# Dense K, Q and output rows, and VectorE's share of the exponentials, in an attention and gated-MLP kernel on one Trainium2 core

## The chip, the cores and the metric

The kernel runs on one core of a Trainium2 chip. The metric is the time on the device, in microseconds (us), of one execution. A profiled execution also leaves a trace with the start and length of every instruction on TensorE (PE), VectorE (DVE), ScalarE (ACT), GpSimd (POOL) and SyncE (SP).

## The reference

A layer of 2048 rows and 640 columns, in bf16: the layer norm of x feeds an attention with 32 heads of 20 columns, and a gated MLP of 1728 columns; both results are joined with x.

```python
xn = layernorm(x)                                       # 2048 x 640
q, k, v = split(xn @ wqkv)                              # 32 heads of Dh = 20
p = softmax(q @ k.T * 20**-0.5)                         # 2048 x 2048 for each head
s = (p @ v).reshape(S, D) @ wo
h = sigmoid(xn @ w_gate) * (xn @ w_up)
g = silu(h @ w_down)
out = x + s * g
```

## The kernel before, in words

**Passes and banks.** The queries are cut into four blocks (`qc`) of 512, the heads into eight groups (`g`) of four. A pair (qc, g) is a pass; there are 32. In a pass, each of the four heads has 16 key tiles of 128, so a pass has 64 banks: a bank is one 128x512 tile of scores, in one bank of PSUM. All 2048 banks must go through an exponential.

The four heads of a group lie on partitions 0, 32, 64 and 96 of `kT_all[:, g, :]` and `qT`, each with 21 rows that count: row 0 carries a bound that is subtracted from the scores, rows 1 to 20 the head's columns. `score` (L874) multiplies 32 rows of the two.

**Who does the exponentials.** `issue` (L928) takes three banks for ScalarE, then two, then three, and so on, in two PSUM sets `sc0` and `sc1`; `act_exp` (L896) turns each such chunk into `p` by one activation (L901). With each chunk one more bank may go to VectorE: `issue` takes one of two PSUM banks (`misc0`, `misc1`, under the name `spare`) if one is free, VectorE's backlog is under 2.5 us (`D_BACKLOG`), and the pass has more than `NEEDED` = 6 banks left (12 in the last pass). `dve_exp` (L906) does that bank in four instructions on 512 columns: `bits` (L912, PSUM to `dy`), `square` (L917, `dy` to `du`), `cube` (L921, `du` to `du`) and `power` (L925, `du` and `dy` to `p`). There is one buffer `du` and two `dy`.

**The other work.** The same two `misc` banks hold the results of all other matmuls (`work`). These are jobs, written as generators:

- `k_job(g, c)`: K of group g, keys of block c: five matmuls with the weights `wkp`, in which each head's 20 columns are padded to 32 (L108); VectorE writes `kT_all` with a 1 in row 0 (L475) and takes the largest magnitude (L121). The last of a group makes the weights of the bound (L118, L115).
- `q_job(qc, g)`: five matmuls with `wqp`, padded in the same way (L143); VectorE takes the magnitudes from PSUM (L127); a sixth matmul adds the bound (L501); VectorE writes `qT` (L506).
- `v_job`, and for the MLP `gateup_job` (L541, L554, tanh on ScalarE L548, product on VectorE L558) and `down_job` (L576).
- `out_job`: the output rows, eight matmuls of 320 columns for each half row tile, one for each group, from `oTs[qc, g]` and the padded `wo_pad` (L614); `part_job` (L646) does the same for six groups of the last query block; the last two groups come at the very end (`out_mm`, L1088).

After a pass, `normalise` copies the sums out of PSUM (L667), sends the denominators through DRAM for the reciprocal (L668 to L684, on POOL's queue) and writes `oT` (L696).

**What sets the order.** The order on every engine is written out by a planner inside the kernel: it keeps a clock for PE (`pe`), queues for ScalarE and VectorE with a cost for each instruction, and a due time (in banks) for each job. `INTO` says what it adds on PE when that engine turns to scores, to PV products or to jobs: 160, 100 and 100 ns. It stops the jobs when the scores are due: `until = max(free, dry - AHEAD) - into`, where `free` is the time at which ScalarE has left the set, `dry` the last moment that keeps ScalarE busy, and `AHEAD` is 80 ns. The chip then runs these orders, each engine in its own, held by semaphores. SP's queue loads `wg`, `wu`, `gqr` and the weights, in program order. When nothing else is due, a multiplication with zeros (`zero_add`) keeps PE running.

Of the kernel before, what the change touches and what calls it, by code (L numbers as in the profile page):

```python
# [14 lines left out]
P = 128  # L15
# [6 lines left out]
V_CHUNKS = ((0, 16), (16, 32))  # L22
OBUFS, WB = 1, 2
# [16 lines left out]
def kernel(  # L40
# [46 lines left out]
    mk_all = const.tile([P, NG, 4], FP32, name="mk_all")  # L87
    mk = const.tile([P, NG], FP32, name="mk")
    bound = const.tile([P, NG, P], BF16, name="bound")
# [7 lines left out]
    wqp = persist.tile([P, KD, HEAD, 32], BF16, name="wqp")  # L97
    wo_pad = persist.tile([P, NG, D], BF16, name="wo_pad")
# [4 lines left out]
    wkp = ep.tile([P, KD, HEAD, 32], BF16, name="wkp")  # L103
    wv = ep.tile([P, KD, D], BF16, name="wv")

    def k_matmuls(ps, g, cols):
        for kd in range(KD):
            nc.tensor.matmul(ps, lhsT=wkp[:, kd, GH * g:GH * g + GH, :].rearrange("p h e -> p (h e)"),  # L108
                             rhs=xnT[:, kd, cols],
                             start=(kd == 0), stop=(kd == KD - 1))  # L110
            yield

    def k_bound(g):
        k_most(g)
        nc.vector.tensor_scalar(out=bound[:, g, :], in0=esum, scalar1=mk[:, g:g + 1], scalar2=None, op0=ALU.mult)  # L115

    def k_most(g):
        nc.vector.tensor_reduce(out=mk[:, g:g + 1], in_=mk_all[:, g, :], axis=AXISX, op=ALU.max)  # L118

    def k_max(src, g, c):  # L120
        nc.vector.tensor_reduce(out=mk_all[:, g, c:c + 1], in_=src, axis=AXISX, op=ALU.max,  # L121
                                apply_absolute_value=True)

    def q_abs(ps):
        absq = wk.tile([P, QC], BF16, tag="absq", bufs=1, name="absq")
        high = ps.bitcast(U16).rearrange("p (q two) -> p q two", two=2)[:, :, 1]
        nc.vector.tensor_scalar(out=absq.bitcast(U16), in0=high, scalar1=0x7FFF, scalar2=None,  # L127
                                op0=ALU.bitwise_and)
        return absq
# [11 lines left out]
    def q_matmuls(ps, cols, g):  # L141
        for kd in range(KD):
            nc.tensor.matmul(ps, lhsT=wqp[:, kd, GH * g:GH * g + GH, :].rearrange("p h e -> p (h e)"),  # L143
                             rhs=xnT[:, kd, cols],
                             start=(kd == 0), stop=(kd == KD - 1))
            yield

    V_SETUP = 4
    qTs = {}
    with tc.tile_pool(name="setup", bufs=1) as sp, \
            tc.tile_pool(name="ps0", bufs=1, space=bass.MemoryType.PSUM) as ps0:
        x_sb = sp.tile([P, TT, D], BF16, name="x_sb")
        wk_raw = sp.tile([P, KD, D], BF16, name="wk_raw")
        wq_raw = sp.tile([P, KD, D], BF16, name="wq_raw")
# [20 lines left out]
        load_w(wk_raw, 1)  # L178
        load_x(12, 4)
        load_w(wq_raw, 0)  # L180
# [7 lines left out]
        nc.vector.memset(wkp[:, :, GH:HEAD, 1 + Dh:32], 0.0)  # L188
        for w in (wkp, wqp):
            nc.gpsimd.memset(w[:, :, 0:GH, 0:1], 0.0)  # L190
            nc.gpsimd.memset(w[:, :, 0:GH, 1 + Dh:32], 0.0)
# [13 lines left out]
        def pad_copy(dst, raw, g0, g1):  # L205
            nc.gpsimd.tensor_copy(
                out=dst[:, :, GH * g0:GH * g1, 1:1 + Dh],
                in_=raw[:, :, GH * g0 * Dh:GH * g1 * Dh].rearrange("p k (h e) -> p k h e", e=Dh))
# [38 lines left out]
        def k_mm(c):  # L247
            kps[c] = ps0.tile([P, 512], FP32, tag="k", bufs=KBUFS, name="ps_k")
            for _ in k_matmuls(kps[c], 0, slice(c * 512, (c + 1) * 512)):
                pass  # L250
# [16 lines left out]
        def q_mm():  # L267
            first["ps"] = ps0.tile([P, 512], FP32, tag="q", bufs=1, name="ps_q")
            for _ in q_matmuls(first["ps"], slice(0, QC), 0):
                pass  # L270

        def q_bound():
            nc.tensor.matmul(first["ps"], lhsT=bound[:, 0, :], rhs=first["abs"], start=False, stop=True,
                             skip_group_check=True)

        def q_evict():
            qT = wk.tile([P, QC], BF16, tag="qT", bufs=2, name="qT")
# [20 lines left out]
        op(("wkp",), "POOL", 0.52, ["wk"], lambda: pad_copy(wkp, wk_raw, 0, 1))  # L298
        ends["wk"], ends["wq"], ends["wv"] = 10.8, 14.7, 16.7
        op(("wqp",), "POOL", 0.52, ["wq"], lambda: pad_copy(wqp, wq_raw, 0, 1))  # L300
        for c in range(4):
            op(("k", c), "PE", 1.3, [("xnT", 4 * c + i) for i in range(4)] + [("wkp",)]
               + ([("kmax", c - KBUFS), ("kadd", c - KBUFS)] if c >= KBUFS else []), lambda c=c: k_mm(c), 0.2)
            op(("kmax", c), "DVE", 0.64, [("k", c)], lambda c=c: k_max(kps[c], 0, c))
            op(("kadd", c), "ACT", 0.57, [("kmax", c)], lambda c=c: k_add(c), 0.6 * (c == 3))
        op(("kmost",), "DVE", 0.2, [("kmax", c) for c in range(4)], lambda: k_most(0))
        op(("kbound",), "ACT", 0.3, [("kmost",)],
           lambda: nc.scalar.activation(out=bound[:, 0, :], in_=esum, func=ACT.Identity, scale=mk[:, 0:1]))
# [30 lines left out]

        nc.gpsimd.memset(wkp[:, :, GH:HEAD, 0:1], 0.0)  # L340
        pad_copy(wkp, wk_raw, 1, 2)
        nc.gpsimd.memset(wqp[:, :, GH:HEAD, 0:1], 0.0)
        nc.gpsimd.memset(wqp[:, :, GH:HEAD, 1 + Dh:32], 0.0)
        pad_copy(wqp, wq_raw, 1, 2)
        pad_copy(wkp, wk_raw, 2, NG)
        pad_copy(wqp, wq_raw, 2, NG)
        nc.gpsimd.memset(v_all[:, :, HH:HEAD, 0:1], 1.0)
        nc.gpsimd.memset(wo_pad.rearrange("p g d -> p (g d)"), 0.0)
# [11 lines left out]
    INTO = {"score": 160.0, "pv": 100.0, "fill": 100.0}  # L360
# [101 lines left out]
    kb_cells = {0: Cell(0.0)}  # L462
# [7 lines left out]
    def k_job(g, c):  # L470
        cols = slice(c * 512, (c + 1) * 512)
        held, ps = yield "bank",
        for _ in k_matmuls(ps, g, cols):
            yield "mm", MM5
        k_cells[g, c] = dve.add(630.0, [Cell(pe[0] + PE_OUT)], lambda: nc.vector.tensor_scalar(  # L475
            out=kT_all[:, g, cols], in0=ps, scalar1=e0[:, 0:1], scalar2=None, op0=ALU.add), 1)
        give_bank(held, k_cells[g, c])
        most = dve.add(620.0, [k_cells[g, c]], lambda: k_max(kT_all[:, g, cols], g, c), 2)
        kb_cells.setdefault((g, "max"), []).append(most)
        if c == 3:  # L480
            kb_cells[g] = dve.add(400.0, kb_cells[g, "max"], lambda: k_bound(g), 2)
# [11 lines left out]
    def q_job(qc, g):  # L493
        yield "known", lambda: kb_cells.get(g)
        held, ps = yield "bank",
        for _ in q_matmuls(ps, slice(qc * QC, (qc + 1) * QC), g):
            yield "mm", MM5
        made = {}
        got = dve.add(600.0, [Cell(pe[0] + PE_OUT)], lambda: made.update(absq=q_abs(ps)), 0)
        yield "wait", [got, kb_cells[g]]  # L500
        nc.tensor.matmul(ps, lhsT=bound[:, g, :], rhs=made["absq"], start=False, stop=True, skip_group_check=True)  # L501
        yield "mm", MM5

        def evict():
            qT = wk.tile([P, QC], BF16, tag="qT", bufs=2, name="qT")
            nc.vector.tensor_scalar(out=qT, in0=ps, scalar1=q_scale, scalar2=e_one[:, 0:1], op0=ALU.mult, op1=ALU.add)  # L506
            qTs[qc, g] = qT

        q_cells[qc, g] = dve.add(600.0, [Cell(pe[0] + PE_OUT)], evict, 0)
        give_bank(held, q_cells[qc, g])  # L510
# [53 lines left out]
    def down_job(tt):  # L564
        c, t4 = divmod(tt, QC // P)
        yield "known", lambda: len(h_cells.get(c, [])) == NFT and (tt < 2 or tt - 2 in gq_cells)
# [22 lines left out]
        def finish():  # L589
            last = c == NQC - 1  # L590
            gq = glu[0].tile([P, D], FP32, tag="gqr", bufs=4, name="gq") if last else d2
# [12 lines left out]
    def out_job(tt):  # L604
# [3 lines left out]
        gqr = glu[0].tile([P, D], FP32, tag="gqr", bufs=4, name="gqr")  # L608
        nc.sync.dma_start(out=gqr, in_=gq_dram[tt, :, :])
        landed = Cell(pe[0] + 3000.0)  # L610
        for h in range(2):
            held, pss = yield "bank",
            for g in range(NG):
                nc.tensor.matmul(pss[:, 0:HALF], lhsT=oTs[qc, g][:, t4 * P:(t4 + 1) * P],  # L614
# [537 lines left out]
```

## Time and profile before

| | us |
|---|---|
| median of three runs before (915.34 to 917.61) | 915.73 |
| the profiled execution | 916.7 |
| its span, first to last instruction | 914.8 |
| from the span's start to the first exponential | 32.4 |
| from the first to the end of the last exponential | 864.3 |
| from there to the end of the span | 18.2 |
| ScalarE busy, in the span | 880.2 |
| VectorE busy, in the span | 837.8 |
| TensorE matmuls busy, in the span | 805.1 |
| mean granted TensorE clock | 0.994 |

A busy share is the union of an engine's instructions. Two instructions of ScalarE overlap at their ends, so what one costs is read from start to start, not from its length. The trace has 1813 banks of scores under the name `sc`, for ScalarE, in 363 chunks of three and 362 of two, and 235 under the name `spare`, for VectorE.

### The profile page before, as it was taken

How to read it: one execution, taken by the hardware profiler on the slowest of the kernel's cores; microseconds unless marked ns; L12 is line 12 of the kernel's file. 1: busy time of each engine (PE TensorE's matmuls, PEld its weight loads, DVE VectorE, ACT ScalarE, POOL GpSimd, SP SyncE). 2: the span in 40 equal slices, each digit the busy share in tenths (PEclk: the TensorE clock that was granted, in tenths of full speed). 3: DMA queues.
4: the chain of work that ended last, by engine and by line, in shares of the span. 5: the costliest groups of instructions: out<-in, count | busy, mean ns of one | idle time of the engine just before them, and what ended most of it. 6: DMA issues, size and time to landing. Idle time of an engine off the chain costs nothing.

```text
span 914.8 us, 16028 instructions
## 1 busy us (share of the span) xinstructions
PE 805.1 (88%) x6027; PEld 274.3 (30%) x6027; DVE 837.8 (92%) x1424; ACT 880.2 (96%) x845; POOL 167.7 (18%) x307
## 2 busy tenths in 40 slices
PE   5898889988888998898889998998899999989995
PEld 2332223322222233322223333222233322223333
DVE  8799999998999999999999999999889967989995
ACT  6989999999999999999999999999999999999992
POOL 7601111011111111211111112111011221011121
PEclk9999999999999999999999999999999999999997
DMA  6070000002222112322221132322102333220003
GB/s 223 22 227 14 13 14 14 2 14 56 49 64 46 32 59 70 51 56 56 57 49 28 52 100 35 66 62 57 38 20 85 79 49 71 45 56 21 13 17 84
DMA packets 91901, 49.50 MB, mean 54 GB/s; under 512 B 78548, under 2 KB 86132, under 8 KB 91696
## 3 DMA queue, kind: packets, MB, share of 16 engines
q1 hardware_dynamic: 81616, 32.37, 14.0%
q0 software_dynamic: 10208, 16.11, 7.8%
q8 instruction: 47, 0.77, 0.3%
q14 instruction: 30, 0.25, 0.1%
HBM read 40.74 MB, written 9.03 MB: 54 GB/s over the span
## 4 chain that ended last, share of the span: by engine, by line
ACT 64%; issue 16%; DVE 10%; PE 8%; DMA 1%; POOL 0%; SPq 0%; DVEq 0%; ACTq 0%; POOLq 0%
ACT p L901 59%; ACT tnh L548 3%; PE sc L879 3%; DVE dy L912 2%; DVE du L917 1%; DVE du L921 1%; PE work L541 1%; DVE p L925 1%; PE oacc L999 1%; DVE stats L214 1%; PE work L133 1%; PE work L554 1%; ACT td L587 1%; DMA x_sb<-in_A_x_dram 0%; PE work L143 0%
## 5 line engine op out<-in xcount | busy, mean ns | idle before, releaser
L901 ACT ACTIVATE p<-sc 128x1536 bf16<-128x1536 f32 x725 | 840.5, 1399 | 6.6 <-PE oacc L999 5.2
L879 PE MATMUL sc<-qT,kT_all 32*128 32x512 bf16 x1813 | 283.1, 382 | 76.7 <-ACT p L901 70.4
L879 PEld LDWEIGHTS <-kT_all 32*128 32x128 bf16 x2048 | 90.9, 90 | 320.0 <-issue 310.3
L912 DVE TENSOR_SCALAR dy<-spare 128x512 f32<-128x512 f32 x235 | 160.8, 684 | 26.0 <-PE spare L879 23.9
L917 DVE SCALAR_TENSOR_TENSOR du<-dy 128x512 f32<-128x512 uint16 x235 | 161.3, 686 | 4.6
L925 DVE SCALAR_TENSOR_TENSOR p<-du,dy 128x512 uint16<-128x512 f32 x235 | 161.0, 685 | 4.0
L921 DVE SCALAR_TENSOR_TENSOR du<-du,dy 128x512 f32<-128x512 f32 x235 | 161.1, 685 | 3.5
L999 PE MATMUL oacc<-p,v_all 128*21 128x512 bf16 x2048 | 157.4, 383 | 0.0
L668 POOL DMA_DIRECT2D den_dram<-oev x31 | 18.0, 582 | 397.1 <-DVE oev L667 387.8
L879 PE MATMUL spare<-qT,kT_all 32*128 32x512 bf16 x235 | 90.1, 383 | 0.0
L576 PE MATMUL work<-wd,hT 128*128 128x320 bf16 x448 | 85.4, 302 | 0.3 <-DVE dy L912 0.2
L541 PE MATMUL work<-xnT,wg 128*128 128x512 bf16 (+1 forms) x280 | 81.2, 383 | 1.0 <-DVE dy L912 0.3
L554 PE MATMUL work<-xnT,wu 128*128 128x512 bf16 (+1 forms) x280 | 76.7, 381 | 1.8 <-DVE dy L912 0.9
L684 POOL DMA_DIRECT2D rl<-rec_dram x124 | 62.1, 513 | 55.0 <-DMA rec_dram<-den 46.4
L576 PEld LDWEIGHTS <-hT 128*128 128x128 bf16 x448 | 35.7, 97 | 46.9 <-issue 35.3
L999 PEld LDWEIGHTS <-v_all 128*21 128x21 bf16 x2048 | 29.7, 90 | 63.3 <-issue 62.3
L143 PE MATMUL work<-xnT,wqp 128*128 128x512 bf16 x155 | 43.9, 382 | 2.5 <-DVE dy L912 2.0
L548 ACT ACTIVATE tnh<-work 128x512 bf16<-128x512 f32 (+1 forms) x56 | 44.3, 791 | 0.0
L558 DVE SCALAR_TENSOR_TENSOR hT<-tnh,work 128x512 bf16<-128x512 bf16 (+1 forms) x56 | 38.0, 679 | 5.4 <-ACT tnh L548 3.9
L678 POOL DMA_DIRECT2D rec_dram<-den x31 | 17.0, 550 | 132.2 <-DVE den L677 132.2
L108 PE MATMUL work<-xnT,wkp 128*128 128x512 bf16 x140 | 39.8, 383 | 0.9 <-DVE dy L912 0.9
L614 PE MATMUL work<-wo_pad,oT 128*128 128x320 bf16 x192 | 36.1, 302 | 0.7 <-DVE dy L912 0.7
(106 smaller groups left out, 556.1 us busy)
## 6 DMA issues: line engine op xcount, KB each, us to landing
wg<-in_B_w_gate_dram SPq DMA_DIRECT2D x52, 160.0 KB
wu<-in_B_w_up_dram SPq DMA_DIRECT2D x52, 160.0 KB
rl<-rec_dram POOLq DMA_DIRECT2D x124, 64.0 KB, 2.3
gq_dram<-d POOLq DMA_DIRECT2D x12, 320.0 KB, 2.5
gqr<-gq_dram SPq DMA_DIRECT2D x12, 320.0 KB
wd<-in_B_w_down_dram SPq DMA_DIRECT2D x1, 2080.0 KB
out_dram<-in_A_x_dram SPq DMA_DIRECT2D x1, 1920.0 KB
out_dram<-gqr POOLq DMA_DIRECT2D x12, 160.0 KB, 3.7
```

The lines of the kernel that those rows point to most:

```text
L541: nc.tensor.matmul(psg[0:fsz, :], lhsT=wg[:, kd, 0:fsz], rhs=xnT[:, kd, cols], start=(kd == 0), stop=(kd == KD - 1))
L548: nc.scalar.activation(out=made["t"][0:fsz, :], in_=psg[0:fsz, :], func=ACT.Tanh, scale=0.5)
L554: nc.tensor.matmul(psu[0:fsz, :], lhsT=wu[:, kd, 0:fsz], rhs=xnT[:, kd, cols], start=(kd == 0), stop=(kd == KD - 1))
L576: nc.tensor.matmul(psd[:, 0:HALF], lhsT=hT[0:fsz, kf, t4 * P:(t4 + 1) * P], rhs=glu[1][0:fsz, kf, e0_:e1_], start=(kf == 0), stop=(kf == N ...
L684: nc.gpsimd.dma_start(out=t["rl"][32 * j:32 * j + 32, :], in_=rec_dram[n, j:j + 1, :].to_broadcast([32, QC]))
L879: nc.tensor.matmul(ps, lhsT=kT_all[32 * j:32 * j + 32, g, kt * P:(kt + 1) * P], rhs=qTs[qc, g][32 * j:32 * j + 32, :], start=True, stop=Tr ...
L901: nc.scalar.activation(out=buf.tile(), in_=ps, func=ACT.Exp, bias=EXP_BIAS, scale=exp_scale)
L912: nc.vector.tensor_scalar(out=t["y"], in0=ps, scalar1=LEAST, scalar2=None, op0=ALU.max)
L917: nc.vector.scalar_tensor_tensor(out=t["u"], in0=t["f"], scalar=CUBE_2, in1=t["f"], op0=ALU.add, op1=ALU.mult)
L921: nc.vector.scalar_tensor_tensor(out=t["u"], in0=t["u"], scalar=CUBE_1, in1=t["f"], op0=ALU.add, op1=ALU.mult)
L925: nc.vector.scalar_tensor_tensor(out=buf.tile()[:, 0, :].bitcast(U16), in0=t["u"], scalar=CUBE_SCALE, in1=t["y"], op0=ALU.mult, op1=ALU.add)
L999: nc.tensor.matmul(oacc[32 * j:32 * j + 1 + Dh, :], lhsT=v_all[:, b % PER_PASS // GH, GH * g + j, 0:1 + Dh], rhs=buf.ap[:, i, :], start=(n ...
```

## The change

K and Q are no longer computed with padded weights for one group at a time. Their columns are computed densely, in five tiles of 128 columns (`DENSE`), turned by 80 columns so that group 0 comes last; group 0 of K and the first Q stay as they were, in the setup. VectorE copies a tile to SBUF, and SP's queue then sends each head's 20 rows to its place, by one DMA for each head or part of a head. The bound is computed for all heads at once, in a bank of its own (`bound_job`), and its row for each group is sent by a further DMA. The output rows are collected in the same way into `ods[qc]`, and multiplied with a dense `wo_all` in five matmuls in place of eight. VectorE has two buffers `du`; the planner's cost for turning to scores is 100 in place of 160; near a pass's end VectorE may take a bank of the next pass, so that the banks are no longer issued in one sequence but by head. `score` multiplies 21 rows in place of 32. Some buffers change: three `oT` in place of twelve, two `gqr` in place of four, three `qT` in place of two. `down_job` of the last block writes into `kT_all`, and waits until its scores have been issued.

```diff
-    def k_job(g, c):
+    def k_job(t, c):
...
-        for _ in k_matmuls(ps, g, cols):
+        for _ in dense_matmuls(ps, wkd, t, cols):
             yield "mm", MM5
...
+            made["k"] = ep.tile([P, 512], BF16, tag="kd", bufs=2, name="kd")
+            nc.vector.tensor_copy(out=made["k"], in_=ps)
+            for h, r, d, n in pieces(t):
+                g, j = divmod(h, GH)
+                if g:
+                    nc.sync.dma_start(out=kT_all[32 * j + 1 + d:32 * j + 1 + d + n, g, cols], in_=made["k"][r:r + n, :])
...
+        kd_free.append(dve.add(606.0, [done], lambda: k_max(made["k"], t, c), 2))
...
+    def q_job(qc, t):
...
+        for _ in dense_matmuls(ps, wqd, t, slice(qc * QC, (qc + 1) * QC)):
             yield "mm", MM5
...
+        qd_cells[qc, t] = dve.add(606.0, [Cell(pe[0] + PE_OUT)], lambda: nc.vector.tensor_scalar(
+            out=qd[:, t, :], in0=ps, scalar1=q_scale, scalar2=None, op0=ALU.mult), 1)
...
+    def bound_job(qc, groups):
...
+                    nc.vector.tensor_scalar(out=made[t].bitcast(U16), in0=qd[:, t, :].bitcast(U16), scalar1=0x7FFF,
+                                            scalar2=None, op0=ALU.bitwise_and)
...
+                nc.tensor.matmul(ps, lhsT=bounds[:, t, :], rhs=made[t], start=(k == 0), stop=(k == len(tiles) - 1))
...
+                nc.vector.tensor_scalar(out=row, in0=ps[0:HEAD, :], scalar1=ONE, scalar2=None, op0=ALU.add)
...
+    def pads():
+        n = next_pad[0]
+        if n == NQC * NG or front() < PER_PASS * (n - 2):
+            return False
...
+        qT = wk.tile([P, QC], BF16, tag="qT", bufs=3, name="qT")
+        for t in TILES[g]:
+            for h, r, d, k in pieces(t):
+                if h // GH == g:
+                    at_row = 32 * (h % GH) + 1 + d
+                    nc.sync.dma_start(out=qT[at_row:at_row + k, :], in_=qd[r:r + k, t, :])
+        row = (g - 1) % NG * GH
+        nc.sync.dma_start(out=qT[0:P:32, :], in_=b_tiles[qc, g][row:row + GH, :])
...
-    INTO = {"score": 160.0, "pv": 100.0, "fill": 100.0}
+    INTO = {"score": 100.0, "pv": 100.0, "fill": 100.0}
...
-            for g in range(NG):
-                nc.tensor.matmul(pss[:, 0:HALF], lhsT=oTs[qc, g][:, t4 * P:(t4 + 1) * P],
-                                 rhs=wo_pad[:, g, h * HALF:(h + 1) * HALF], start=(g == 0), stop=(g == NG - 1))
+            for k in range(KD):
+                nc.tensor.matmul(pss[:, 0:HALF], lhsT=ods[qc][:, k, t4 * P:(t4 + 1) * P],
+                                 rhs=wo_all[:, k, h * HALF:(h + 1) * HALF], start=(k == 0), stop=(k == KD - 1))
...
+            for h in range(GH * g, GH * g + GH):
+                a = h * Dh
+                while a < (h + 1) * Dh:
+                    b = min((h + 1) * Dh, (a // P + 1) * P)
+                    at_row = 32 * (h % GH) + 1 + a - h * Dh
+                    nc.sync.dma_start(out=ods[qc][a % P:a % P + b - a, a // P, :], in_=oT[at_row:at_row + b - a, :])
+                    a = b
...
-    K_DUE, Q_DUE, V_DUE, OUT_DUE = -40, -24, 6, 4 * PER_PASS
+    K_DUE, Q_DUE, B_DUE, V_DUE, OUT_DUE = -60, -50, -36, 6, 4 * PER_PASS
...
+    def dve_bank(banks):
+        b = min((x for x in coming(GH) if x not in banks), default=None)
+        if b is None:
+            return None
+        left = PER_PASS - b % PER_PASS
+        if left > (NEEDED if b < NB - PER_PASS else NEEDED_LAST):
+            return b
+        if b >= NB - PER_PASS:
+            return None
+        b = PER_PASS * (b // PER_PASS + 1) + b % GH
+        while b // GH in done_ahead[b % GH]:
+            b += GH
+        cells = [w[0].get(w[1]) for w in needs(b)]
+        if any(c is None or c.t is None or c.t > pe[0] for c in cells):
+            return None
+        return b
...
-            t["u"] = pp.tile([P, 512], FP32, tag="du", bufs=1, name="du")
+            t["u"] = pp.tile([P, 512], FP32, tag="du", bufs=2, name="du")
...
-        first = dve.add(600.0, [Cell(begun + MM5 + PE_OUT - 100.0), *d_made[-2:-1]], bits, 0)
-        c = dve.add(610.0, [first, *d_made[-1:]], square, 3)
-        c = dve.add(610.0, [c], cube, 3)
-        buf.made = dve.add(610.0, [c, buf.before], power, 3)
+        first = dve.add(606.0, [Cell(begun + MM5 + PE_OUT - 100.0), *d_made[-2:-1]], bits, 0, 114.0)
+        c = dve.add(606.0, [first, *d_made[-2:-1]], square, 3, 114.0)
+        c = dve.add(606.0, [c], cube, 3, 114.0)
+        buf.made = dve.add(606.0, [c, buf.before], power, 3, 114.0)
...
-        if (ci > 1 and b % PER_PASS < PER_PASS - (NEEDED if b < NB - PER_PASS else NEEDED_LAST) and dve.backlog + max(0.0, dve.t - pe[0]) < D_BACKLOG
+        if (ci > 1 and dve.backlog + max(0.0, dve.t - pe[0]) < D_BACKLOG
                 and all(c.t is not None for c in d_made[-2:-1])):
-            split = take_bank("spare")
+            extra = dve_bank(taken)
+            if extra is not None:
+                split = take_bank("spare")
```

## Prediction

> **What bounds the kernel now.** I read the page first: the engines' shares, the chain that ended last, the costliest groups.
>
> ```profile
> PE 805.1 (88%) x6027; PEld 274.3 (30%) x6027; DVE 837.8 (92%) x1424; ACT 880.2 (96%) x845; POOL 167.7 (18%) x307
> ...
> ACT 64%; issue 16%; DVE 10%; PE 8%; DMA 1%; POOL 0%; SPq 0%; DVEq 0%; ACTq 0%; POOLq 0%
> ...
> L901 ACT ACTIVATE p<-sc 128x1536 bf16<-128x1536 f32 x725 | 840.5, 1399 | 6.6 <-PE oacc L999 5.2
> L879 PE MATMUL sc<-qT,kT_all 32*128 32x512 bf16 x1813 | 283.1, 382 | 76.7 <-ACT p L901 70.4
> ...
> L912 DVE TENSOR_SCALAR dy<-spare 128x512 f32<-128x512 f32 x235 | 160.8, 684 | 26.0 <-PE spare L879 23.9
> ```
>
> ScalarE is busy 96% of the span, and of its exponentials only 6.6 us are waited for. Of 2048 banks ScalarE does 1813 and VectorE 235; TensorE waits 70.4 us for ScalarE, not the other way. So the end comes earlier only by fewer banks on ScalarE, that is more on VectorE, which is itself busy 92%.
>
> ScalarE's price is read from start to start in its timeline: 1.331 us for a chunk of three banks, 0.904 for one of two, so 2.235 for five, 0.447 a bank. 1813 x 0.447 = 810.4; 56 tanh of the gates at 0.478 and 16 of the down rows at 0.627 add 36.8; the first to the last exponential takes 864.3, which leaves 17.1 of small stalls. With n banks on VectorE, **ScalarE's time is (2048 - n) x 0.447 + 53.9**.
>
> VectorE's price is in its timeline (start, length, line, operation):
>
> ```profile
> 400.12 0.69 DVE L917 SCALAR_TENSOR_TENSOR du<-dy 128x512 f32<-128x512 uint16 x1
> 400.73 0.68 DVE L912 TENSOR_SCALAR dy<-spare 128x512 f32<-128x512 f32 x1
> 401.33 0.68 DVE L921 SCALAR_TENSOR_TENSOR du<-du,dy 128x512 f32<-128x512 f32 x1
> 402.05 0.69 DVE L925 SCALAR_TENSOR_TENSOR p<-du,dy 128x512 uint16<-128x512 f32 x1
> 402.78 0.69 DVE L917 SCALAR_TENSOR_TENSOR du<-dy 128x512 f32<-128x512 uint16 x1
> 403.50 0.69 DVE L921 SCALAR_TENSOR_TENSOR du<-du,dy 128x512 f32<-128x512 f32 x1
> 404.11 0.68 DVE L558 SCALAR_TENSOR_TENSOR hT<-tnh,work 128x512 bf16<-128x512 bf16 x1
> ```
>
> The next instruction starts after 0.61 us where it has nothing to do with the one before (L917, then L912 of another bank), after 0.72 where it needs its result (L921 to L925), and also from a power to the next square (402.05 to 402.78), since both use the one `du`. Over the exponential phase the starts give: 613.9 us for the 235 banks (2.612 each; four steps at 0.603 would be 2.412, so 0.200 a bank is dependence), 203.1 for everything else, 48.5 of gaps. Together 865.5, against a phase of 864.3; I carry the 1.2 as an edge. **VectorE's time is n x 2.612 + 203.1 + 48.5 - 1.2**. Setting the two equal gives n = 235.1 and 864.4: the two engines are balanced, and the sum below uses this pair.
>
> **VectorE's other work.** Groups by form, with length and, from the timeline, start to start:
>
> ```profile
> L506 DVE TENSOR_SCALAR qT<-work,e_one 128x512 bf16<-128x512 f32 x31 | 23.1, 744 | 1.7 <-PE work L501 1.6
> ...
> L127 DVE TENSOR_SCALAR absq<-work 128x512 uint16<-128x512 uint16 x31 | 21.0, 677 | 0.1
> L475 DVE TENSOR_SCALAR kT_all<-work,e 128x512 bf16<-128x512 f32 x28 | 20.8, 742 | 0.0
> L121 DVE TENSOR_REDUCE mk_all<-kT_all 128x1 f32<-128x512 bf16 x28 | 18.9, 676 | 0.0
> ```
>
> - Removed: K 28 x (0.659 + 0.596) = 35.1; Q 31 x (0.600 + 0.662) = 39.1; weights of the bound 7 x (0.183 + 0.168) = 2.5. Sum 76.7.
> - Added: K 20 x (0.600 + 0.596) = 23.9 (five tiles, four blocks; a plain copy, priced as L667's 0.600); Q 20 x 0.600 = 12.0; the bound's rows, 5 + 3 evictions, 8 x 0.600 = 4.8; weights 5 x 0.351 = 1.8; magnitudes 9 + 15 = 24. These are now read from SBUF in 16 bits. No row shows that form: the ends are 0.168 (L115, a quarter of the columns) and 0.600 (L127, from PSUM); I take 0.25, near the first, which is also from SBUF: 6.0, ends 4.0 and 14.4. Sum 48.5.
> - Left of "everything else": 203.1 - 76.7 + 48.5 = 174.9.
>
> **Two square tiles.** With two `du`, a power no longer holds the next square, and the steps of two banks can alternate; one or two banks are always pending at a backlog limit of 2.5 us. Ends: all of the 0.200 a bank stays (2.612), none (2.412). I take a quarter left, 2.46, since now and then only one bank is there. [...]
>
> **VectorE's gaps.** 48.5 us, and they are concentrated:
>
> ```profile
> 700.00:740.00 40.00, 36.61 (x296) 13.31 (x288) 38.41 (x65) 40.00 (x38) 8.50 (x14) 1.00 0.26 62
> 740.00:780.00 40.00, 37.34 (x259) 11.11 (x257) 24.48 (x40) 40.00 (x39) 7.27 (x14) 1.00 0.33 65
> ```
>
> From 740 to 780 us VectorE (third figure) is busy 24.5 of 40 us while TensorE is at 37.3: the jobs hold both `misc` banks, and no spare is left. TensorE's work falls: K 140 to 100 matmuls, Q 186 to 100 + 24, 102 fewer at 0.216 (start to start within one job), 22.0; output rows 192 to 120 and 48 to 32, 88 fewer at 0.135, 11.9; 34 us. The bank of the next pass fills the last six banks, in which VectorE got few (of 235, two in the last four banks of all passes, about 15 in each other four). Ends: 48.5 (nothing) and 20; I take 33.
>
> **Later scores.** Turning to scores really takes 312 ns from the start of the last 512-column matmul to the first score; less 216 for that matmul is 96, so a cost of 100 is right and 160 had TensorE arrive 60 ns early. That reserve goes. From a set's release to the score are at least 50 ns, from there to its exponential at least 495; an exponential of three lies 1.612 in the engine, so it can be back after 2.157 us, and 2.235 is its turn: 78 ns to spare for chunks of three, some 500 for chunks of two. Ends: 0, and 60 ns on all 363 chunks of three, 21.8 us. I take 3, near the first, as 78 covers 60.
>
> **SP's queue** gets some 450 DMAs: K 128, Q 36 x 4 less 4 with the setup's group, and 31 rows, output rows about 140, 7 rows of ones, 9 for `wo`. The nearest rows are the 32 loads of `wo_pad`, also 20 rows each:
>
> ```profile
> 37.71 11.90 SPq L754 DMA_DIRECT2D wo_pad<-in_A_wo_dram  x32
> ...
> den_dram<-oev POOLq DMA_DIRECT2D x31, 8.0 KB, 1.7
> den<-den_dram POOLq DMA_DIRECT2D x31, 8.0 KB, 2.0
> ```
>
> 0.372 us each to issue, some 2 to land: 167 us of a queue that is idle for most of the span. A pass's query rows (six DMAs) take 6 x 0.372 + 2 = 4.2 us; `pads` sends them up to two passes (54 us) ahead, at a new query block after the bound, due 36 banks (15 us) ahead. The loads of `wg` and `wu` ahead of them in the queue wait for matmuls that TensorE has been given earlier, so they hold them by a few us. Cost 0; if that cover goes, scores wait by what exceeds the lead.
>
> **Start and end.** The setup's chain to the first exponential at 32.4 us keeps its steps: 0. After the last exponential, VectorE's timeline still shows four evictions of `part_job` until 899.4, and the last copy of the sums (L1080) right behind, 899.3; with 32 in place of 48 of its matmuls these end sooner: between 0 and 1.7, I take 1.0.
>
> **The sum.** (2048 - n) x 0.447 + 53.9 + 3 = 2.46 n + 174.9 + 33 - 1.2, so n = 263.4 and the phase 854.7: 9.7 less than 864.4. With 1.0 at the end 10.7. The profiled execution took 916.7 (span 914.8, 1.9 around it): 906.0. It stands 1.0 above the median, so against that I forecast **905.0 us**.
>
> **The rivals.**
>
> 1. *Interleaving buys nothing*: each step keeps its 2.612. For it: two banks are not always pending, and a quarter of VectorE's instructions already lie between steps. Against: 0.61 us in the lines above. n = (972.5 + 1.2 - 207.9)/3.059 = 250.3, phase 860.6, 4.8 less: 911. Chance 0.15.
> 2. *VectorE is filled*: no dependence left, gaps of 20, no cost of later scores, ScalarE's stalls 12. (964.4 + 1.2 - 194.9)/2.859 = 269.6, phase 843.9, with the end 22 less: 894. Chance 0.11. For it: the planner sees the dependence, and has 34 us more of TensorE.
> 3. *Later scores* (slower): ScalarE runs dry at the chunks of three, as TensorE loses its 60 ns. With 21.8 for 3, n = 269.9 and the phase is 870.6, 6.2 more: 921. Of each us more, 0.85 stays after the rebalance, so it decides from 3 + 10.7/0.85 = 15.6 us, 43 ns a chunk. For it: 78 ns of room is little. Against: TensorE waits 70.4 us for ScalarE now. Chance 0.11.
> 4. *Not as said*: the small DMAs, in one queue with the weights, reach some passes late, and banks are held; at 0.3 us a pass, 9 us, the gain is gone: 915. Chance 0.05.
>
> **How the numbers follow.** My forecast has 0.58. About 0.3% (2.7 us) is what a measurement here can tell from no change. Faster by more: the forecast, rival 2, and four fifths of rival 1, 0.58 + 0.11 + 0.12 = 0.81; within it: the rest of rival 1 and most of rival 4, 0.07; slower: rival 3 and what is left, 0.12. The range goes from rival 2 (893) to just below no change (914); above that lies rival 3, outside.
>
> **What would show it.** `spare` should be near 263 (250: rival 1; 270: rival 2). Square to cube and cube to power should mostly start after 0.60. VectorE's "everything else" should be near 175 us, and the stretch after 740 should be filled. If ScalarE's idle time before L901 or its starts above 0.904 and 1.331 add up to much over 20 us, rival 3 holds; if scores wait for DMAs at a pass's start, rival 4. The forecast is wrong if VectorE is freed and doesn't get banks.

## The result and the profile after

The changed kernel takes **980.45 us** (median of four executions, 974.46 to 991.91) against 915.54 before: a ratio of 1.068 (95% interval 1.063 to 1.073; it leaves out the longest execution, which stands apart from the other three). 905 was forecast, with 914 as the upper end. TensorE's granted clock is 0.940 in the shortest execution and 0.921 in the longest, against 0.994 before. The profiled execution took 974.46, its span is 972.5.

The page of the changed kernel: busy time of the engines; the granted clock, in tenths, in 40 slices; the chain that ended last; ScalarE's and VectorE's exponentials; the scores of the spares; the multiplications with zeros; and the eviction of K.

```profile
PE 826.4 (85%) x5942; PEld 267.9 (28%) x5942; DVE 852.0 (88%) x1497; ACT 872.3 (90%) x835; POOL 158.9 (16%) x306
...
PEclk9889659998999999999999979999969998999997
...
ACT 45%; issue 16%; DVE 14%; PE 14%; SPq 6%; DMA 4%; DVEq 0%; POOL 0%; ACTq 0%; POOLq 0%
...
L1050 ACT ACTIVATE p<-sc 128x1536 bf16<-128x1536 f32 x715 | 827.8, 1347 | 75.5 <-PE sc L1027 56.6
...
L1061 DVE TENSOR_SCALAR dy<-spare 128x512 f32<-128x512 f32 x261 | 178.3, 683 | 42.3 <-PE spare L1027 39.9
...
L1027 PE MATMUL spare<-qT,kT_all 21*128 21x512 bf16 x261 | 103.1, 395 | 17.9 <-DVE kd L487 15.1
...
L1138 PE MATMUL oacc<-xnT,zero 128*128 128x512 bf16 x164 | 55.4, 387 | 0.0
...
L487 DVE CAST kd<-work 128x512 bf16<-128x512 f32 x20 | 13.7, 686 | 34.6 <-DMA kT_all<-kd 15.8
```

VectorE does 261 banks; 263 were forecast. This is a number of the planner, which has laid down every engine's order before the chip runs; it does not show that the engines kept to the plan's times. ScalarE, which waited for 6.6 us before its exponentials, now waits for 75.5; SP's queue and the DMAs, 0% and 1% of the chain before, are 10% of it. From the first to the last exponential 924.5 us pass, 60.2 more than before. Taken apart by ScalarE's starts: the exponentials themselves cost 797.9 in place of 809.1 (11.2 less), idle time before them in that phase is 74.3 in place of 5.5 (68.8 more), and 2.6 is the rest. After the phase 16.0 us remain in place of 18.2. The planner also fills TensorE with 164 multiplications with zeros in place of 59: 105 more, some 22 us at 0.213 each (the start to start of PV products of 512 columns in both traces), of the 34 us that were to be set free.

By pass (the copy of the sums out of PSUM marks a pass's end): the third pass ends at 165.3 us in place of 119.0, the sixth is 8 us longer than before, and the 18th, 24th and 27th each lose about 4 to 6 more. In between, VectorE's banks bring back a little. SP's queue in the first passes (start, length, line, operation):

```profile
40.14 21.14 SPq L491 DMA_DIRECT2D kT_all<-kd  x28
61.38 2.98 SPq L592 DMA_DIRECT2D qT<-qd  x4
64.47 0.56 SPq L594 DMA_DIRECT2D qT<-row  x1
84.08 27.71 SPq L491 DMA_DIRECT2D kT_all<-kd  x36
111.84 3.69 SPq L592 DMA_DIRECT2D qT<-qd  x5
```

A DMA of 20 rows from SBUF to SBUF costs this queue 21.14/28 = 0.755 us, twice the 0.372 of the `wo_pad` loads. The planner keeps no time for this queue: it counts K as landed 3.4 us (`DMA_WAIT`, L365) after its eviction (L492), however many DMAs stand ahead. 116 of K's 128 have been issued by 166 us. The query rows of the second pass come behind K's first tile. VectorE has two buffers `kd` and must wait until the DMAs have read one; its order is laid down, so its exponentials and the banks that it holds wait too. The waits of the changed kernel (engine and line, what was waited for: us in total, times, longest):

```profile
ACT p L1050 <- PE sc L1027: 56.6, 21, 10.4
...
DVE kd L487 <- DMA kT_all<-kd: 15.8, 5, 6.7
PE spare L1027 <- DVE kd L487: 15.1, 3, 7.7
...
DVE kd L487 <- DMA od<-oT: 12.2, 1, 12.2
...
PE sc L1027 <- DMA qT<-row: 7.7, 1, 7.7
```

Few and long: 21 waits of ScalarE make 56.6 us.

### The profile page after: what moved, and what is told of

It reads as the page before. It is cut to its first block, busy times and chain, and to the rows that moved or that the text cites. A ratio compares the mean times of both kernels' runs of the same rounds, so it can differ in the third digit from the quotient of the medians.

```text
span 972.5 us, 16664 instructions
## 1 busy us (share of the span) xinstructions
PE 826.4 (85%) x5942; PEld 267.9 (28%) x5942; DVE 852.0 (88%) x1497; ACT 872.3 (90%) x835; POOL 158.9 (16%) x306
## 4 chain that ended last, share of the span: by engine, by line
ACT 45%; issue 16%; DVE 14%; PE 14%; SPq 6%; DMA 4%; DVEq 0%; POOL 0%; ACTq 0%; POOLq 0%
ACT p L1050 40%; PE sc L1027 4%; SPq L491 3%; DVE dy L1061 3%; ACT tnh L636 3%; PE oacc L1153 3%; DVE du L1070 2%; DVE du L1066 2%; PE work L665 2%; DVE p L1074 2%; PE work L629 1%; PE work L120 1%; SPq L592 1%; DMA gqr<-gq_dram 1%; DMA kT_all<-kd 1%
## 5 line engine op out<-in xcount | busy, mean ns | idle before, releaser
L1050 ACT ACTIVATE p<-sc 128x1536 bf16<-128x1536 f32 x715 | 827.8, 1347 | 75.5 <-PE sc L1027 56.6
L1027 PE MATMUL sc<-qT,kT_all 21*128 21x512 bf16 x1787 | 286.0, 393 | 82.8 <-ACT p L1050 70.0
L1061 DVE TENSOR_SCALAR dy<-spare 128x512 f32<-128x512 f32 x261 | 178.3, 683 | 42.3 <-PE spare L1027 39.9
L1027 PEld LDWEIGHTS <-kT_all 21*128 21x128 bf16 x2048 | 91.1, 91 | 332.5 <-issue 314.7
L1070 DVE SCALAR_TENSOR_TENSOR du<-du,dy 128x512 f32<-128x512 f32 x261 | 177.7, 682 | 2.0
L1074 DVE SCALAR_TENSOR_TENSOR p<-du,dy 128x512 uint16<-128x512 f32 x261 | 177.6, 681 | 1.7
L1066 DVE SCALAR_TENSOR_TENSOR du<-dy 128x512 f32<-128x512 uint16 x261 | 177.5, 682 | 0.9
L1027 PE MATMUL spare<-qT,kT_all 21*128 21x512 bf16 x261 | 103.1, 395 | 17.9 <-DVE kd L487 15.1
L1138 PE MATMUL oacc<-xnT,zero 128*128 128x512 bf16 x164 | 55.4, 387 | 0.0
L487 DVE CAST kd<-work 128x512 bf16<-128x512 f32 x20 | 13.7, 686 | 34.6 <-DMA kT_all<-kd 15.8
L769 POOL DMA_DIRECT2D rec_dram<-den x31 | 17.1, 551 | 147.9 <-DVE den L768 147.9
L642 PEld LDWEIGHTS <-wu 128*128 128x128 bf16 (+1 forms) x280 | 24.0, 99 | 45.5 <-issue 32.3
```

Source lines behind the costliest of these rows:

```text
L642: nc.tensor.matmul(psu[0:fsz, :], lhsT=wu[:, kd, 0:fsz], rhs=xnT[:, kd, cols], start=(kd == 0), stop=(kd == KD - 1))
L1027: nc.tensor.matmul(ps, lhsT=kT_all[32 * j:32 * j + 1 + Dh, g, kt * P:(kt + 1) * P], rhs=qTs[qc, g][32 * j:32 * j + 1 + Dh, :], start=True, ...
L1050: nc.scalar.activation(out=buf.tile(), in_=ps, func=ACT.Exp, bias=EXP_BIAS, scale=exp_scale)
L1061: nc.vector.tensor_scalar(out=t["y"], in0=ps, scalar1=LEAST, scalar2=None, op0=ALU.max)
L1066: nc.vector.scalar_tensor_tensor(out=t["u"], in0=t["f"], scalar=CUBE_2, in1=t["f"], op0=ALU.add, op1=ALU.mult)
L1070: nc.vector.scalar_tensor_tensor(out=t["u"], in0=t["u"], scalar=CUBE_1, in1=t["f"], op0=ALU.add, op1=ALU.mult)
```

## The experiments

**The theory** after the result: small DMAs fill SP's queue in the first four passes, later single rows come late, and a stall is made longer where TensorE's clock halves behind it, as from 43.7 to 57.4 us of the changed kernel (0.50). **The rivals:** the bytes or the DMA engines themselves; the order of the banks or the later scores (rival 3 of the prediction). "Before" below is that kernel's time on the same chip in the same group of runs.

### K gathered, 32 DMAs in place of 128 (a_merge)

```diff
+            if c == 0:
+                kds[t] = ep.tile([P, S], BF16, tag="kd", bufs=2, name="kd")
+            nc.vector.tensor_copy(out=kds[t][:, cols], in_=ps)
+            if c < 3:
+                return
...
+                    nc.sync.dma_start(out=kT_all[32 * j + 1 + d:32 * j + 1 + d + n, g, :], in_=kds[t][r:r + n, :])
```

The planner's due times for K follow the tile in place of the block.

> The changed kernel, with K of one tile gathered over the four key blocks and sent by one DMA for each head, 32 in place of 128, the same bytes. Theory (SP's issue time, 0.75 us for each of 128): 96 x 0.75 = 72 us of SP's queue go from the first four passes, so most of the 52 us that these passes lost come back: 925 to 945. Rival (bytes, or TensorE's clock, or the order of banks): 970 or more, as the bytes and the order are the same.

939.27 us, ratio to before 1.0255 (1.0227 to 1.0283). 41 of the 65 us are gone with the same bytes and the same 261 banks. The third pass now ends 3.1 us after that of before, not 46. SP's queue in this kernel:

```profile
42.59 5.29 SPq L495 DMA_DIRECT2D kT_all<-kd  x7
47.99 2.98 SPq L597 DMA_DIRECT2D qT<-qd  x4
```

A DMA with four times the bytes costs the queue the same 0.756 us (5.29/7): between these two sizes the price is by DMA. The theory holds for the first passes.

### K's DMAs on POOL's queue (a_pool)

```diff
-                    nc.sync.dma_start(out=kT_all[32 * j + 1 + d:32 * j + 1 + d + n, g, cols], in_=made["k"][r:r + n, :])
+                    nc.gpsimd.dma_start(out=kT_all[32 * j + 1 + d:32 * j + 1 + d + n, g, cols], in_=made["k"][r:r + n, :])
```

> The changed kernel, with the 128 DMAs of K issued on POOL's queue in place of SP's. Theory: SP is free for Q and the output rows, POOL issues at its own price (0.5 to 0.6 us in the rows of normalise), so at least half of the loss in the first passes goes: 930 to 955; normalise, which shares POOL's queue, may be late by some us. Rival (bytes or the DMA engines limit): 970 or more.

940.87 us, one execution. With all 128 DMAs, on another queue, the total is close to that of the gathering, but the gain does not lie in the same place: the third pass still ends 19.9 us after that of before, against 3.1 in a_merge and 46.4 in the changed kernel. POOL's queue is the cheaper one for this DMA (start, length, line, operation):

```profile
98.62 16.03 POOL L491 DMA_DIRECT2D kT_all<-kd  x32 [2.44 <-DVE kd L487]
```

That is 0.50 us each, and VectorE still waits 5.3 us for these DMAs before it can write `kd`. Moving them takes back 26 of the 46 us that the first three passes lose, by a queue of their own and by a lower price, which this run does not separate; gathering them takes back 43. The time to issue is not small here: 0.755 us on SP, where the 8 KB of `den_dram` on POOL's queue, in the kernel before, take 1.7 from issue to landing; and the kernel waited for it.

### The same DMAs where nobody waits (b_scrap)

```diff
+    for n in range(128):
+        r = 32 * (n % 4) + 1
+        nc.sync.dma_start(out=scrap[r:r + Dh, n // 4 % 2, :], in_=kT_all[r:r + Dh, 0, 0:512])
```

> The kernel before, with 128 DMAs of 20 rows of 1 KB from SBUF to SBUF put into SP's queue after the loads of wo: copies of a part of K into a scrap tile that nobody reads. Theory (their issue on one queue costs 0.71 us each, and hurts only where somebody waits): SP's queue shows 128 x 0.75 = 96 us of them, and the time is that of before within 2 us. Rival (their bytes or the DMA engines slow the kernel by themselves): 5 us or more over before.

917.95 us, ratio 1.0027 (1.0008 to 1.0045). SP's queue has them as

```profile
49.14 96.75 SPq L1022 DMA_DIRECT2D scrap<-kT_all  x128
```

0.756 us each, at a cost of about 1 us to the kernel. The price belongs to this form of DMA on this queue, and hurts only through those who wait. The loads for the MLP, behind the 128 in the queue, are issued at 146 to 153 us in place of 50 to 56, and this too costs little here.

### VectorE's part alone (b_du, b_into, b_next, b_inext, b_all2)

All from the kernel before, without dense projections. b_du and b_all2 also have the change's costs for VectorE in the planner; b_next, b_inext and b_all2 have three `qT` buffers. With all three parts and twelve `oT` buffers (b_all) the kernel does not fit into SBUF and has no time; b_all2 has eleven.

```diff
# b_du, b_all2
-            t["u"] = pp.tile([P, 512], FP32, tag="du", bufs=1, name="du")
+            t["u"] = pp.tile([P, 512], FP32, tag="du", bufs=2, name="du")
# b_into, b_inext, b_all2
-    INTO = {"score": 160.0, "pv": 100.0, "fill": 100.0}
+    INTO = {"score": 100.0, "pv": 100.0, "fill": 100.0}
# b_next, b_inext, b_all2: dve_bank, coming, issued as in the change
```

> The kernel before with only the second square tile and VectorE's costs in the planner. Dependence lost a VectorE bank 0.200 us in before; theory: most of it goes, VectorE takes 5 to 12 banks more, the time is 2 to 6 us under before. Rival (interleaving buys nothing, as each instruction waits for the one before it anyway): 235 banks, the time of before within 1 us.

> The kernel before with only the planner's cost of turning to scores at 100 in place of 160. Theory: the measured turn is 96, TensorE loses no time that ScalarE needed, and gets room for spares: 236 to 245 banks on VectorE, 912 to 917. Rival (later scores): ScalarE idles more before its exponentials, over 920.

> The kernel before with only the bank of the next pass near a pass's end (and three qT buffers). Theory: VectorE's four steps are in balance with ScalarE already, so a few banks more at most, 235 to 242, 912 to 917. Rival (the order by head costs): over 920.

> The kernel before with the cost of 100 for turning to scores and the bank of the next pass, one square tile. Theory: of the three parts, these two pay (6.4 and 2.3 us alone), and the second square tile doesn't pay by itself (3.5 us slower alone); together 905 to 910, at or under the 909.2 of all three. Rival (the second tile pays once there is room for spares): over 911.

> The kernel before with only VectorE's and the planner's part of the change: two square tiles, the cost of 100 for turning to scores, the bank of the next pass, three qT buffers (and eleven oT buffers in place of twelve, for room). Theory (the loss is SP's queue of small DMAs and what it triggers): none of it is here, so the time is within 8 us of before, 910 to 921, and TensorE's clock stays at full. Rival (order of banks, later scores): 950 or more, with ScalarE idle before its exponentials by 50 us.

| | us | ratio to before (95%) | banks | VectorE us a bank | its gaps, us |
|---|---|---|---|---|---|
| before | 916 to 917 | | 235 | 2.612 | 48.5 |
| b_du | 920.22 | 1.0036 (1.0023 to 1.0049) | 232 | 2.515 | 79.2 |
| b_into | 910.54 | 0.9936 (0.9920 to 0.9953) | 236 | 2.618 | 40.8 |
| b_next | 914.68 | 0.9977 (0.9968 to 0.9987) | 241 | 2.615 | 29.2 |
| b_inext | 910.32 | 0.9936 (0.9920 to 0.9953) | 241 | 2.618 | 25.5 |
| b_all2 | 909.17 | 0.9918 (0.9900 to 0.9936) | 243 | 2.505 | 46.9 |

Order of banks and later scores are not the cause: with both, and the second tile, the kernel is 0.8% *faster* than before, the lowest ratio of all, though its interval overlaps those of b_into and b_inext. b_into alone brings 6 us, more than its expectation said, so the reserve of 60 ns was a loss, not a cover. Of the page of b_into:

```profile
L901 ACT ACTIVATE p<-sc 128x1536 bf16<-128x1536 f32 x725 | 836.5, 1362 | 4.9 <-PE oacc L999 2.9 <-POOL wqp L206 1.2 <-PE sc L879 0.8
L879 PE MATMUL sc<-qT,kT_all 32*128 32x512 bf16 x1812 | 282.5, 382 | 62.7 <-ACT p L901 57.1
```

ScalarE waits less than before (4.9 in place of 6.6 us). One bank more would be worth 0.447 us; the rest of the 6.3 us between the two spans comes by other ways: 3.1 us lie between the first and the last exponential, nearly all of it less idle time of ScalarE, 2.4 behind the last one, where 12 matmuls of `part_job` are left over in before and none here, and 0.9 ahead of the first. With this number in place the bank of the next pass adds five banks and no time that these runs can tell (b_inext and b_into have the same ratio).

The second tile does half of what it could to a bank (2.515 in place of 2.612, with 2.412 as the floor) and gains nothing by itself: VectorE's waits for the scores of a spare grow from 23.9 to 34.5 us. So b_du bears out neither its theory nor its rival. Of the 3.6 us by which b_du's span is longer, 2.0 lie behind the last exponential, with 26 matmuls of `part_job` left over there, and 2.1 ahead of it, with three banks more on ScalarE. Why the planner gave VectorE fewer banks wasn't settled, and b_inext at 910.32 decides neither for its theory nor for its rival.

### TensorE's clock (b_nozero)

```diff
-    WINDOW, ENOUGH = 3400.0, 2300.0
+    WINDOW, ENOUGH = 3400.0, 0.0
```

The kernel before without its 59 multiplications with zeros; they add nothing to the result.

> The kernel before without the 59 multiplications with zeros; no small DMA, nothing else changed. Theory: in the traces so far TensorE's clock halves after a stretch of 3.4 us in which it streamed less than about 0.45 of the time; without the zeros some stretches fall below that, so half-clock stretches appear in the middle of the kernel, each costs some us, 920 to 950. Rival (the half clock comes from stalls for DMAs, not from little work): clock full, time of before within 2 us.

926.62 us, ratio 1.0111 (1.0076 to 1.0147). The profiled execution is the longest of four, 930.66. Stretches of this kernel (from:to, length, then busy time of TensorE, its weight loads, VectorE, ScalarE and POOL with instruction counts, the granted clock, the DMA share, GB/s):

```profile
255.80:259.20 3.40, 2.06 (x21) 0.58 (x20) 3.33 (x6) 3.40 (x5) 0.55 (x1) 0.96 0.00 0
259.20:269.40 10.20, 9.45 (x44) 1.82 (x43) 6.72 (x11) 7.34 (x7) 1.98 (x4) 0.51 0.19 45
269.40:272.90 3.50, 3.21 (x26) 0.84 (x23) 3.30 (x6) 3.31 (x3) 0.00 (x0) 1.00 0.21 47
```

TensorE is busy 2.06 of 3.40 us without any stall for a DMA, then its clock is 0.51 for 10.2 us, and ScalarE idles for 2.9 of them. In the changed kernel's trace the nine stretches at 0.50 before the last exponential take 3.41, 6.83, 10.24, 13.65, 17.07 or 37.55 us, multiples of 3.41. Cut into stretches of 3.41 us, with a 512-column matmul counted as 0.213 us of streaming and concurrent ones once, the sixteen traces show between the first and the last exponential: all 31 stretches at full clock that streamed under 0.41 of their time were followed by half clock, none over 0.51 was, and of the 82 between them 16 were. What decided among those 82 was not shown. So TensorE need not stand still: from 709.3 to 712.7 us of the changed kernel it was busy for 1.89 us and streamed 0.39 of the time, and half clock followed for 17.07 us.

### What is left in the changed kernel (a_zero, a_fix, a_fixz, a_fixm, a_fixp)

All from a_merge, which loses 9.8 us of ScalarE's time in the sixth pass and some 5 at the 18th, 24th and 27th. The stretches of a_merge in the sixth pass, and VectorE's wait in it:

```profile
179.70:183.10 3.40, 2.62 (x23) 0.77 (x22) 3.40 (x7) 3.40 (x5) 0.00 (x0) 1.00 1.03 359
183.10:186.50 3.40, 3.02 (x28) 0.88 (x27) 1.69 (x3) 3.40 (x4) 0.56 (x1) 1.00 1.11 413
186.50:189.90 3.40, 0.39 (x3) 0.19 (x3) 0.00 (x0) 2.29 (x3) 0.00 (x0) 0.99 0.97 399
189.90:207.00 17.10, 14.84 (x62) 2.79 (x61) 10.75 (x21) 8.57 (x8) 2.53 (x5) 0.50 0.21 52
...
190.12 0.25 DVE L773 RECIPROCAL den<-den 128x16 f32<-128x16 f32 x1 [5.34 <-DMA den<-den_dram]
```

The big loads for the MLP fill the DMA engines (share about 1, 400 GB/s); VectorE waits 5.3 us for `den`, which goes through DRAM; TensorE falls to 0.39 of 3.40 us, and then has half its clock for 17.1. In the kernel before SP's queue was idle and issued these loads at 50 to 56 us, long before they were needed; now they stand in the queue behind all of K's DMAs, the last of which is issued at 165.3 us, and go out at 177 to 179. In b_scrap they go out at 147 to 149, also beside such a round trip, and VectorE waits 2.3 us for it; why less than in a_merge wasn't settled.

```diff
# a_fix, a_fixz, a_fixm, a_fixp: w_down and x to out in 25 pieces, 3.5 us apart; gqr one tile ahead
...
+        for n, fn in enumerate(first):
+            at(pe[0] + 3500.0 * n, fn)
...
+        if t4 < 3:
+            load_gqr(tt + 1)
# a_zero, a_fixz (2800.0); a_fixm, a_fixp (3400.0)
-    WINDOW, ENOUGH = 3400.0, 2300.0
+    WINDOW, ENOUGH = 3400.0, 2800.0
# a_fixp: output rows on POOL's queue
-                    nc.sync.dma_start(out=ods[qc][a % P:a % P + b - a, a // P, :], in_=oT[at_row:at_row + b - a, :])
+                    nc.gpsimd.dma_start(out=ods[qc][a % P:a % P + b - a, a // P, :], in_=oT[at_row:at_row + b - a, :])
```

> The variant with K gathered (939 us), in which the planner adds multiplications with zeros until TensorE has 2800 of 3400 ns in place of 2300. Theory: its half-clock stretches (54.6 us) begin where TensorE has too little to do, since work was taken from it; so those without a stall ahead of them go (at 674 us, 17 us long) and the time falls by 3 to 10 us. Rival (the half clock only follows stalls for a DMA, at 190, 528 and 762 us): stretches and time stay as they are, within 2 us.

> The variant with K gathered, in which also the big loads at the MLP's start (w_down, the copy of x to the output) are cut in 25 pieces 3.5 us apart, and the rows of the MLP for the output (gqr) are asked for one tile earlier. Theory: the stall of 9.8 us in the sixth pass is the denominators' way through DRAM behind those loads, and those of some 5 us at the 18th and 27th pass are gqr behind the small DMAs; so 15 to 20 of the 23 us over before go: 917 to 926. Rival (these stalls come from the clock or the order of banks): 935 or more.

> Both: the pieces and the earlier gqr, and zeros up to 2800 of 3400 ns. Theory: no stall and no half clock is left, VectorE's 261 banks are worth 11 us, so it comes out below the kernel before, 903 to 914. Rival (the gain of VectorE is eaten elsewhere): 916 or more.

> The variant with K gathered, the big loads in pieces and gqr earlier, in which the planner fills every free slot of TensorE with zeros (3400 of 3400 ns). Theory (what is left over before is the half clock, since TensorE has too little to do): half-clock stretches shrink to under 10 us, the runs agree with each other, and the time is 905 to 917. Rival (stalls for rows that come by DMA are left, and zeros can't fill a stall in TensorE's own queue): runs stay apart, 920 to 940.

> The same, with the 140 DMAs of the output rows issued on POOL's queue in place of SP's. Theory: 105 us of SP's queue go, query rows and gqr come earlier, so stalls at the start of a query block shrink; 903 to 915, below the one without it. Rival: POOL's queue, with the denominators in it, is late in its place, and the time is no better or worse.

| | us | ratio to before (95%) | banks | ScalarE idle, us | half clock, us |
|---|---|---|---|---|---|
| a_merge | 939.27 | 1.0255 (1.0227 to 1.0283) | 261 | 36.1 | 54.6 |
| a_zero | 940.66 | 1.0244 (1.0204 to 1.0285) | 256 | 38.5 | 58.0 |
| a_fix | 920.35; three from 937.32 to 939.22 | none | 255 | 19.6 | 30.7 |
| a_fixz | 927.07 | 1.0111 (1.0070 to 1.0151) | 261 | 28.9 | 17.0 + 30.7 at the end |
| a_fixm | 921.43 | 1.0046 (1.0028 to 1.0065) | 259 | 19.1 | 10.2 |
| a_fixp | 926.86 | 1.0118 (1.0096 to 1.0139) | 259 | 26.4 | 34.1 |

(The last two columns, and the banks, are of the profiled execution: 935.79 for a_merge, 942.01 for a_zero, 931.08 for a_fixz, 919.33 for a_fixm and 928.04 for a_fixp.) a_fix was profiled at 920.35, with a clock of 0.979, and its other three executions took 937 to 939 at 0.950 to 0.954. In its trace the wait for `den` is gone; VectorE still waits 3.3 us for `gqr` at 737 us, but ScalarE has no wait over 1.5 us there. Of the other three only times and clocks are on record, so what made them long stays open beyond their lower clock. a_zero missed: its half clock stays (58.0 us, 54.6 in a_merge), mostly behind stalls, where zeros can't run, since they stand in the same queue. With the big loads in pieces as well, a_fixz takes 927 and a_fixm 921 us; both miss their expectations (903 to 914 and 905 to 917). The ten executions of a_fixm lie at 916.98 to 923.77, the shortest at a clock of 0.998. So the zeros alone gain nothing; the pieces alone reach a_fixm's time in one execution of four; with both, no execution of a_fixm is as long as those three. "Too little work" (b_nozero) and "stalls" (a_merge) are two ways into the same half clock. a_fixp missed: POOL's queue is no better place for the output rows; VectorE still waits for `gqr` at 322 and 742 us, 3.6 and 2.5 us.

a_fixm is still 0.5% over before, 5 us, with 24 banks more on VectorE. In its trace ScalarE idles 13.6 us more than before: 5.7 more in the first two passes, the rest in small pieces. What the last ones wait for wasn't settled.

## Why the prediction was wrong

- **SP's queue: the step that failed.** "0.372 us each to issue ... Cost 0" is wrong twice. The price was taken from loads out of DRAM with the same 20 rows, and is 0.756 from SBUF to SBUF (b_scrap, by itself); the number of DMAs, 450, was right. And the lead was worked out for query rows alone. 116 of K's 128 DMAs fall into the first four passes, 88 us of the queue at their price where four passes took some 110 before, and hold what stands behind: query rows, VectorE by its two `kd`, the MLP's loads. Gathering them brought 41 us back (a_merge), moving them some 40, in one execution (a_pool). Rival 4 named the mechanism, at 9 us and a chance of 0.05, a seventh of the 65 that it cost. Of the 23 us left over in a_merge, the pieces, the earlier `gqr` and the zeros took all but 5 (a_fixm); how the 65 divide between waiting and half clock was not separated.
- **TensorE's 34 us: a benefit on paper.** They were counted only as room for spares, and the planner gave some 22 of them to zeros. In before the zeros keep the clock (0.994; without them, in b_nozero, it is 0.976 and the time 1.1% longer); with less work and now and then a stall it halves all the same, 105.8 us of the phase in the changed kernel, 54.6 in a_merge, against none before. The prediction has no step for the clock.
- **VectorE's other work: right.** 174.9 us forecast, 174.9 measured. That it is right to the tenth is luck: the magnitudes, for which 0.25 us was chosen, cost 0.20 from start to start.
- **Two square tiles: near in size, wrong in worth.** 2.46 a bank forecast, 2.494 measured. The timeline of the changed kernel shows it:

```profile
639.82 0.68 DVE L1061 TENSOR_SCALAR dy<-spare 128x512 f32<-128x512 f32 x1
640.42 0.68 DVE L1074 SCALAR_TENSOR_TENSOR p<-du,dy 128x512 uint16<-128x512 f32 x1
641.02 0.68 DVE L1066 SCALAR_TENSOR_TENSOR du<-dy 128x512 f32<-128x512 uint16 x1
641.74 0.69 DVE L1070 SCALAR_TENSOR_TENSOR du<-du,dy 128x512 f32<-128x512 f32 x1
642.35 0.68 DVE L1061 TENSOR_SCALAR dy<-spare 128x512 f32<-128x512 f32 x1
```

Three of four steps now start 0.60 us apart; only the cube still follows its own square, 0.72. Rival 1, by which 2.612 would stay, falls. But alone the tile gained nothing (b_du), so the sum that turned every us of VectorE into banks is too simple: a bank must also be free.

- **VectorE's gaps: wrong sign.** 33 forecast, 99.0 measured. In a_merge, with fewer stalls and the same banks, VectorE idles 38 us less, so the stalls make up much of it.
- **Later scores: wrong sign.** 3 us of cost forecast; alone the smaller number gains 6 (b_into). Rival 3 falls. The prediction also held that the end comes earlier only by fewer banks on ScalarE, and took its 17.1 us of small stalls as fixed; b_into gains its 6 us with one bank fewer on ScalarE, by less idle time and a shorter end.
- **Banks:** 263 forecast, 261 measured, worth 11.2 us of ScalarE. The sum set the number by VectorE's time; here the planner set it, and it is the same in a_merge and a_pool, with gaps that differ. That 261 came out beside gaps three times as large is no support for the sum.
- **The end:** 1.0 us less forecast, 2.2 measured. No matmul of `part_job` is left over behind the last exponential, as was meant; but b_into has that too, and 2.4 us, with all 48 of them, so the dense rows are not shown to be its cause.

The prices of the two balanced engines' work came out, their waits did not; what failed was an engine at 0% of the chain, whose queue the change filled, and which the planner does not see.

## What to carry to other kernels

Before many small DMAs go onto one queue, multiply their number by the issue time of that very form, and set it against the stretch in which they are due, not against the span; look at who stands behind them in order, on the queue and on the engine that waits for their buffers. Work taken from an engine that isn't the bound cost its clock here (0.976 in place of 0.994 without 59 multiplications, b_nozero): look how busy it is in the emptiest stretches. Where a planner lays down the order, ask which queues it has no clock for. Take the parts of a change one by one: here one number in the planner was worth 0.6% without the rest.

## What was not expected of the hardware

- Issuing a DMA of 20 rows: 0.33 us on SP from DRAM to SBUF, 0.71 (0.756 from start to start) from SBUF to SBUF, for rows of 1 KB or of 4 KB alike; 0.50 from SBUF to SBUF on POOL's queue (a_pool).
- TensorE's clock halved after each of the 31 stretches of 3.41 us that streamed under 0.41 of the time, after 16 of the 82 between 0.41 and 0.51, and after none above (sixteen traces). In the changed kernel it then stayed halved for one to eleven such stretches, 3.41 to 37.55 us. In three of them, 10.2 us, ScalarE idled for 2.9 (b_nozero).
- About 4 MB asked for at one time (`w_down` with 2080 KB, `x` to the output with 1920) held up the denominators' round trip through DRAM (8 KB): 12.2 us in a_merge and 9.3 in b_scrap, some 7 in most other passes.
